# An attention and gated-MLP kernel whose written order follows rules with fixed numbers: the numbers now change stage by stage by a table

## The chip, the cores and the metric

The kernel runs on one core of a Trainium2 chip. Times are device microseconds; the profile is one profiled execution of the whole program. A core has five engines with queues of their own: PE (TensorE, matrix products), DVE (VectorE), ACT (ScalarE), POOL (GpSimd) and SP (SyncE, which here only starts transfers). Each runs its instructions in the order in which they were written and waits for the others by semaphores.

## The reference, cut to what matters

```python
# S = 2048, D = 512, H = 32 heads of 16, F = 1376, everything bf16
g = sigmoid((x * gate_w).sum(-1, keepdims=True))
qkv = (x @ wqkv)                       # split into q, k, v, 32 heads each
p = softmax(q @ k.T * 16 ** -0.5)      # per head, 2048 x 2048
a = (p @ v, heads joined) @ wo
b = ((x @ w_gate) * (x @ w_up)) @ w_down
out = g * a + (1 - g) * b
```

The softmax has 32 x 2048 x 2048 exponentials, which is what most of the kernel's work hangs on. There is no maximum taken off; the sums of the exponentials come out of the same products as the values, from a column of ones beside each head's values.

## The kernel before, in words

**Units.** The scores are cut into 2048 units of 128 keys x 512 queries of one head. They come in 32 groups `m` (8 times four heads, for each of 4 chunks of 512 queries), each of 16 key tiles times 4 heads. One unit fills one PSUM bank of 128 x 512. `score` (L1191) issues its four small matmuls of 64 rows x 32 columns (L1237), on the upper or the lower half of the rows of PE's array; two such packs on the two halves run beside each other.

**Two ways to take the exponential.** A unit is of kind "a" or "d", which `score` decides when it issues it.

- Kind "a": ACT reads the bank and writes bf16 exponentials to a cell of the SBUF tile PT (L1332, in `act_policy`, L1283). One pass takes two units where two neighbouring banks are ready, and else one.
- Kind "d": DVE adds a constant to the bank and writes int16 (L1474, in `dve_pass`, L1446). The score is scaled so that the integer's bits, read as bf16, are a coarse exponential. To make it finer the unit's cell is copied three times with an integer offset each (SH = 0, 32, 64, 96): on POOL (L1411) or on DVE (L1414), both in `run_shift` (L1395), for 512, 1024 or 2048 elements of a partition at once. The four cells are each multiplied with their own scaled copy of the values (CW), so that a "d" unit costs four times the value matmuls of an "a" unit.

**The value products.** `pv_pack` issues four matmuls of 64 rows x 32 columns (L1776) that add exponentials times values into one PSUM bank per group. When a group is complete, its bank is copied out, the sums are inverted and brought back by small transfers, and POOL multiplies (L1693) into OT.

**Fills.** All other products (transposing x, the projections k, q, v, the gate and up projections, the down projection, the output projection; L563, L567, L601) are "fills": they go to PE where it would otherwise not have work, and DVE takes their results out of PSUM. Cells of PT are used first for weights and x, later for exponentials as they come free.

**Who sets the order.** A planner runs when the program is written. It keeps a clock of its own with a fixed duration for each kind of instruction, and when an engine is free by that clock it asks the engine's policy (`dve_policy`, `act_policy`, `pool_policy`, `pe_policy`, `sp_policy`) for its next instruction. What is issued is put at the end of the engine's queue; the waits follow from the data. The chip knows nothing of the planner's clock; it only gets the order. The policies compare with numbers. Among those that the change touches:

- TA and TLO: up to how much ACT work is queued may PE issue a score for ACT, and below how much is "a" preferred to "d";
- DTH, DTH2, RQ, CD, DE, DK: how much DVE work may be queued, and how many cells must be free, for a "d" unit to be issued, and near which end of a group none is;
- AB, DB: which of the 8 PSUM banks are for "a" (below AB) and for "d" and fills (from DB);
- GM: with how many units ACT may make a pass, in which order they are tried; AW: how long ACT may wait for a second unit;
- WIN, SKEW: how far the scores may be taken out of order, and how far one half of PE may lead the other;
- CQ, CQ1, PW, SPL: when DVE takes a shift copy itself, when POOL does, and when a copy is split;
- CL, FP, PB, PL, PACE2, AHEAD, FB, EV, RES: when a fill goes ahead of the value products, how far one half leads in them, and when DVE empties a bank ahead of an exponential.

The last group's sums, the last product with wo and the output stand behind the planner's loop in a fixed order (L1998 to L2083).

## Time and the profile before

| | |
|---|---|
| median of 3 runs | 711.08 us (711.0 to 711.76) |
| the profiled execution | 711.66 us |
| its span in the trace | 709.9 us |
| granted clock of PE | 1.00 |
| PE, ACT, DVE, POOL busy | 99%, 97%, 92%, 60% of the span |

Busy time counts an instruction from its start to its end; where two overlap, as successive instructions on one engine do, the shared time counts once. "PEld" is the loading of PE's weights. A line such as "L1332 ACT ACTIVATE ... x740 | 684.6, 1055 | 9.3 <-..." gives a group's count, its busy time in us, the mean of one in ns, and the time for which the engine stood idle just before instructions of the group, with what ended it.

### The profile page before, as it was taken

What the parts mean: (1) busy time and instruction counts of PE and PEld (TensorE: products, weight loads), DVE (VectorE), ACT (ScalarE), POOL (GpSimd) and SP (SyncE); (2) the same over time, 40 slices, a digit from 0 to 9 for tenths busy, and PEclk for the clock granted to TensorE, in tenths of its full rate; (3) what the DMA queues carried; (4) which work ended last, traced back from release to release, by engine and by line L of the source; (5) the groups of instructions that cost most, each with busy time, mean ns of one, the idle gap of its engine ahead of it and who ended that gap; (6) DMA issues with size and microseconds to landing.
All of it is one profiled execution on the core that took longest, in us unless ns stands there. A gap on an engine that the chain in (4) does not pass through costs nothing.

```text
span 709.9 us, 47002 instructions
## 1 busy us (share of the span) xinstructions
PE 700.3 (99%) x21872; PEld 385.8 (54%) x21872; DVE 656.4 (92%) x1160; ACT 691.8 (97%) x757; POOL 429.4 (60%) x326
## 2 busy tenths in 40 slices
PE   8999999999999999999999999999999999999997
PEld 5555555555555556545555564545555555555553
DVE  5788999998999999999999999999999999998994
ACT  6989999999999999999999999999999999999997
POOL 3124767767455767456667477776546777772671
PEclk9999999999999999999999999999999999999999
DMA  8300111312012222212005221111104311120001
GB/s 248 80 9 9 28 26 36 72 38 57 23 27 50 66 68 46 53 38 62 22 9 120 48 54 34 31 53 37 46 6 96 83 38 57 38 73 9 16 19 39
DMA packets 77619, 34.86 MB, mean 49 GB/s; under 512 B 60784, under 2 KB 74480, under 8 KB 77424
## 3 DMA queue, kind: packets, MB, share of 16 engines
q1 hardware_dynamic: 76480, 31.34, 18.0%
q8 instruction: 171, 2.80, 1.6%
q10 hardware_dynamic: 944, 0.52, 0.2%
q14 instruction: 24, 0.20, 0.1%
HBM read 25.23 MB, written 2.35 MB: 39 GB/s over the span
## 4 chain that ended last, share of the span: by engine, by line
PE 91%; DVE 5%; DMA 1%; ACT 1%; SPq 1%; issue 1%; DVEq 0%
PE ps L1237 32%; PE ps L1776 31%; PE ps L567 27%; DVE PT L1474 2%; DMA gw<-in_gate_w_dram 1%; ACT PT L1332 1%; DVE PT L1414 1%; SPq L450 1%; PE ps L563 0%; DVE omg L834 0%; DVE KT L642 0%; DVE usb L918 0%; DVE VV L758 0%; PE ps L601 0%; PE ps L784 0%
## 5 line engine op out<-in xcount | busy, mean ns | idle before, releaser
L1332 ACT ACTIVATE PT<-ps 128x1024 bf16<-128x1024 f32 x741 | 685.1, 1054 | 9.3 <-PE ps L1237 4.3
L1776 PE MATMUL ps<-PT,VV 64*32 64x512 bf16 x7498 | 552.9, 377 | 1.1
L1411 POOL TENSOR_SCALAR PT<-PT 128x1024 int16<-128x1024 int16 (+1 forms) x284 | 395.7, 1410 | 209.1 <-DVE PT L1414 84.4
L1237 PE MATMUL ps<-QT,KT 64*32 64x512 bf16 x8192 | 477.4, 379 | 2.9 <-DVE PT L1474 1.1
L567 PE MATMUL ps<-PT 64*32 64x512 bf16 x5536 | 390.5, 377 | 0.4 <-DVE VV L758 0.2
L1474 DVE TENSOR_SCALAR PT<-ps 128x512 int16<-128x512 f32 x567 | 369.9, 683 | 14.8 <-PE ps L1237 9.5
L1776 PEld LDWEIGHTS ps<-PT,VV 64*32 64x32 bf16 x7498 | 189.0, 92 | 87.4 <-PE ps L1776 12.4
L1237 PEld LDWEIGHTS ps<-QT,KT 64*32 64x32 bf16 x8192 | 140.3, 89 | 152.2 <-ACT PT L1332 61.3
L567 PEld LDWEIGHTS ps<-PT 64*32 64x32 bf16 x5536 | 134.5, 92 | 64.7 <-DVE PT L1474 9.7
L1414 DVE TENSOR_SCALAR PT<-PT 128x2048 int16<-128x2048 int16 (+1 forms) x290 | 159.8, 594 | 5.8 <-PE ps L1776 5.1
L567 PE MATMUL ps<-wo,OT 64*32 64x512 bf16 x480 | 37.4, 377 | 0.1
L748 POOL TENSOR_SCALAR VV<-VV 128x528 bf16<-128x528 bf16 x17 | 10.7, 631 | 39.6 <-DVE VV L758 35.0
L933 DVE TENSOR_TENSOR PT<-ps,usb 128x512 bf16<-128x512 f32 (+1 forms) x44 | 30.0, 681 | 2.6 <-PE ps L567 2.5
L918 DVE CAST usb<-ps 128x512 bf16<-128x512 f32 (+1 forms) x44 | 30.0, 681 | 2.1 <-PE ps L567 2.1
L1693 POOL TENSOR_TENSOR OT<-oraw,rb 128x512 bf16<-128x512 f32 x16 | 20.5, 1278 | 18.4 <-DVE PT L1414 18.4
L1715 DVE COPY oraw<-ps 128x512 f32<-128x512 f32 x31 | 21.1, 682 | 1.0 <-PE ps L1776 0.9
L758 DVE CAST VV<-ps 128x512 bf16<-128x512 f32 x16 | 10.8, 688 | 7.3 <-PE ps L567 7.2
L567 PEld LDWEIGHTS ps<-wo,OT 64*32 64x32 bf16 x480 | 12.0, 92 | 7.0 <-DVE PT L1474 1.3
L642 DVE CAST KT<-ps 128x512 bf16<-128x512 f32 x16 | 11.0, 685 | 4.4 <-PE ps L1776 1.9
L982 DVE TENSOR_SCALAR bsb<-ps,omg 128x512 bf16<-128x512 f32 x16 | 11.9, 743 | 0.2 <-PE ps L567 0.2
L699 DVE TENSOR_SCALAR QR<-ps 128x512 bf16<-128x512 f32 x16 | 10.9, 683 | 0.5 <-PE ps L567 0.5
L626 DVE CAST PT<-ps 128x512 bf16<-128x512 f32 x14 | 8.9, 683 | 2.6 <-PE ps L601 2.6
(51 smaller groups left out, 78.8 us busy)
## 6 DMA issues: line engine op xcount, KB each, us to landing
PT<-in_B_w_up_dram SPq DMA_DIRECT2D x40, 128.0 KB, 3.0
PT<-in_B_w_gate_dram SPq DMA_DIRECT2D x40, 128.0 KB, 3.3
PT<-in_B_w_down_dram SPq DMA_DIRECT2D x20, 256.0 KB, 3.3
rb<-rscr SPq DMA_DIRECT2D x15, 256.0 KB
QT<-QR SPq DMA_DIRECT2D x124, 16.0 KB, 2.0
oraw<-oraw SPq DMA_DIRECT2D x60, 32.0 KB, 2.0
out_dram<-ost SPq DMA_DIRECT2D x14, 128.0 KB, 2.1
PT<-in_A_x_dram SPq DMA_DIRECT2D x3, 512.0 KB, 7.4
```

The lines of the kernel that those rows point to most:

```text
L567: o = pe.matmul(ps[32 * i : min(w, 32 * i + 32), bank, :], lhs(32 * i, min(w, 32 * i + 32))[q], rhs[q], start=s0, stop=s1, tile_position=( ...
L918: lambda v: v.tensor_copy(usb[0:w, n % 2, :], ps[0:w, bank, :]),
L933: lambda v: v.tensor_tensor(hT[0:w, f, :], ps[0:w, bank, :], usb[0:w, n % 2, :], ALU.mult),
L982: lambda v: v.tensor_scalar(bsb[:, tt, :], ps[:, bank, :], omg[:, t : t + 1], None, ALU.mult),
L1237: o_ = pe.matmul(ps[32 * i_ : 32 * i_ + 32, x, :], KT[64 * r : 64 * r + 64, b, kt * 128 + 32 * i_ : kt * 128 + 32 * i_ + 32], QT[64 * r : ...
L1332: lambda a: a.activation(span(PT, cs).bitcast(BF16), span(ps, bs), ACT.Exp, scale=ESC),
L1411: fn = lambda e: e.tensor_scalar(dst, src, 1.0, sh, ALU.mult, ALU.add)
L1414: fn = lambda e: e.tensor_single_scalar(dst, src, sh, ALU.add)
L1474: lambda v: v.tensor_scalar(span(PT, cs), span(ps, bs), IOFF, 0.0, ALU.add, ALU.max),
L1693: lambda g: g.tensor_tensor(OT[:, pair % 6, :], oraw[:, 0, :], rb[:, :], ALU.mult),
L1715: lambda v: v.tensor_copy(oraw[:, p, :], ps[:, bank, :]),
L1776: o_ = pe.matmul(ps[32 * j : 32 * j + 32, ob, :], v_ap(k, kt, 8 * b + 2 * j + p, p)[rows], PT[rows, cell, :].bitcast(BF16), start=f0, stop ...
```

## The change

The numbers that were constants of `_build` become attributes of an object `kn`, read by the same policies at the same places. A table TUNE lists, for times of the planner's clock, which of them take another value from then on; there are 59 entries from 10 to 670, and the loop applies them as its clock passes. No instruction is added to the kernel's repertoire, no tile, transfer or bank is added, and the planner's durations are the same. Its line numbers are 67 higher behind the table (L1332 becomes L1399), and 71 higher behind the loop.

```diff
-    DTH = 1.2
-    CQ = 3
...
+    kn = _Knobs()
+    kn.CD = 2
+    kn.DTH = 1.2
...
+    TUNE = [
+        (10.0, {"CL": 8, "FP": 1, "AB": 4, "DB": 3}),
+        (20.0, {"CQ": 6}),
+        (30.0, {"CD": 4}),
+        (40.0, {"DTH": 1.6, "WIN": 4, "CL": 12}),
+        (50.0, {"CD": 2, "DTH": 1.2, "WIN": 2, "CQ": 3, "FP": 0, "AB": 4, "DB": 4}),
+        (60.0, {"PB": 2, "EV": 1}),
+        (80.0, {"PL": 4, "AHEAD": 400}),
+        (90.0, {"DE": 3, "RES": 6}),
+        (100.0, {"CD": 1, "SPL": 12, "AHEAD": 80, "GM": (2,)}),
...
+        (300.0, {"CD": 0, "CQ1": 2, "PL": 8, "SKEW": 3}),
...
+        (360.0, {"CQ": 2, "CQ1": 2, "DE": 2, "SKEW": 3, "TLO": 0.6, "TA": 1.3, "FP": 1}),
...
+        (410.0, {"CD": 2, "WIN": 2, "CL": 12, "SKEW": 2, "TLO": 0.6, "TA": 1.6, "SPL": 12, "EV": 0, "GM": (3, 2, 1), "DK": 6}),
...
+        (590.0, {"DTH": 1.2, "DTH2": 0.6, "PW": 0.5, "AW": 0, "WIN": 2, "SKEW": 4, "TLO": 0.6, "TA": 2.0, "EV": 0}),
...
+        (650.0, {"PACE2": 0.95, "AB": 4, "DB": 3}),
+        (670.0, {"FP": 0}),
+    ]
+    seg = 0
...
         def high(fb):
-            return [x for x in fb if x >= DB]
+            return [x for x in fb if x >= kn.DB]
...
             t = heapq.heappop(events)
             while events and events[0] <= t + 1e-9:
                 heapq.heappop(events)
+            while seg < len(TUNE) and t >= TUNE[seg][0]:
+                for k_, v_ in TUNE[seg][1].items():
+                    setattr(kn, k_, v_)
+                seg += 1
             moved = True
```

The instructions of the two built programs differ in these counts; all others are the same:

| | before | after |
|---|---|---|
| ACT exponential, two units a pass / one unit | 740 / 1 | 727 / 6 |
| DVE exponential, one unit / two units | 567 / 0 | 584 / 2 |
| PE value matmuls (L1776) | 7498 | 7624 |
| DVE shift copies of 2048 / 1024 / 512 elements (L1414) | 158 / 126 / 6 | 151 / 132 / 4 |
| POOL shift copies of 2048 / 1024 / 512 elements (L1411) | 122 / 161 / 1 | 141 / 164 / 0 |

## The prediction

> **What bounds the kernel now.** I read the page's first part, the chain of waits, the groups by form, the waits of single engines, the busy time by stretch, and the timeline of the end.

> ```profile
> span 709.9 us, 47002 instructions
> PE 700.3 (99%) x21872; PEld 385.8 (54%) x21872; DVE 656.4 (92%) x1160; ACT 691.8 (97%) x757; POOL 429.4 (60%) x326
> PE 91%; DVE 5%; DMA 1%; ACT 1%; SPq 1%; issue 1%; DVEq 0%
> ```

> Three engines look full, and the chain of waits gives 91% of the span to PE. Both readings need testing. First the groups by form, with the count, the busy time and the mean of one:

> ```profile
> L1332 ACT ACTIVATE PT<-ps 128x1024 bf16<-128x1024 f32 x740 | 684.6, 1055 | 9.3 <-PE ps L1237 4.3 <-PE ps L1776 4.0 <-PE ps L567 0.4
> L1474 DVE TENSOR_SCALAR PT<-ps 128x512 int16<-128x512 f32 x567 | 369.9, 683 | 14.8 <-PE ps L1237 9.5 <-PE ps L1776 1.4 <-PE ps L567 0.2
> L1411 POOL TENSOR_SCALAR PT<-PT 128x2048 int16<-128x2048 int16 x122 | 231.2, 1898 | 107.1 <-DVE PT L1414 77.3 <-PE ps L1776 14.1 <-PE ps L1237 10.9
> L1411 POOL TENSOR_SCALAR PT<-PT 128x1024 int16<-128x1024 int16 x161 | 166.8, 1045 | 102.0 <-DVE PT L1474 71.9 <-PE ps L1776 15.4 <-DVE PT L1414 7.1
> L1414 DVE TENSOR_SCALAR PT<-PT 128x2048 int16<-128x2048 int16 x158 | 105.4, 691 | 0.7 <-PE ps L1776 0.4
> L1414 DVE TENSOR_SCALAR PT<-PT 128x1024 int16<-128x1024 int16 x126 | 59.3, 487 | 5.1 <-PE ps L1776 4.7
> ```

> ACT does almost nothing but the exponential: 740 passes over two score units each and one over a single unit, that is 1481 of the 2048 units; DVE's L1474 does the other 567. A pair takes 1055 ns, but successive passes overlap, so that each adds only 684.6/740 = 0.925 us.

> Now the stretches (time, PE, PEld, DVE, ACT, POOL busy with counts):

> ```profile
> 30.00:40.00 10.00, 10.00 (x359) 5.69 (x340) 7.54 (x20) 10.00 (x12) 1.26 (x2) 1.00 0.02 6
> 40.00:50.00 10.00, 9.66 (x300) 5.05 (x292) 9.57 (x23) 8.59 (x10) 2.91 (x5) 1.00 0.04 10
> 50.00:60.00 10.00, 10.00 (x324) 4.98 (x312) 6.50 (x16) 8.35 (x10) 0.87 (x2) 1.00 0.02 4
> 100.00:650.00 550.00, 547.49 (x17620) 304.41 (x17609) 528.36 (x912) 548.17 (x594) 358.97 (x257) 1.00 0.20 49
> 500.00:550.00 50.00, 50.00 (x1684) 28.41 (x1678) 48.36 (x85) 49.92 (x56) 26.89 (x20) 1.00 0.22 52
> ```

> From 100 to 650 us ACT is idle for 1.8 us of 550. PE is "busy" as well, but with 17620/550 = 32.0 matmuls per us, while between 30 and 40 us it did 35.9 and in the densest steady stretch 33.7. So PE has 5 to 12% left in the steady part. Who waits for whom says the same:

> ```profile
> PEld ps L1237 <- ACT PT L1332: 61.3, 278, 0.8
> ACT PT L1332 <- PE ps L1237: 4.3, 7, 1.2
> ACT PT L1332 <- PE ps L1776: 4.0, 5, 1.4
> ```

> The score matmuls wait 61.3 us for ACT to free a PSUM bank; ACT waits 8.7 us in all for PE (0.4 of it for L567, in the first group row). ACT is the bound, PE is what ACT's release sets going, and the chain runs through PE because each PE instruction has a predecessor there.

> **The change part by part.** The edit itself alters only numbers that the scheduler reads when the program is written; what changes on the chip is the order and four counts. They come from the order of instructions of the two built programs. Everything is made against the profiled execution, 711.66 us with a span of 709.9; it lies 0.58 above the median of 711.08.

> 1. *Units moved from ACT to DVE.* ACT's pair passes go from 740 to 727 and its single passes from 1 to 6, so 1460 units are left; DVE's go from 567 to 588 (584 single ones and two double ones). Thirteen pairs at 0.925 give -12.0 us. Five singles cost between half a pair, 0.46, and the whole duration of the only single one:

> ```profile
> L1332 ACT ACTIVATE PT<-ps x741: 673/1043/1180, 9.2 to 702.1; 128x1024 bf16<-128x1024 f32 x185, 128x512 bf16<-128x512 f32 x1
> ```

> That is 0.673. A pair overlaps its neighbour by 1.055 - 0.925 = 0.13, so I take 0.673 - 0.13 = 0.54, and +2.7 for five. Sum -9.3 us; bounds -8.7 (0.673 each) and -12.0 (singles free). Nearly all of it lies on the path, since in the steady part ACT has no idle time that would absorb it. [...]

> 2. *The start.* Four of the new singles are passes 33 to 40 of ACT. In the trace this is just ahead of ACT's only real starvation:

> ```profile
> 25.33 22.24 ACT L1332 ACTIVATE PT<-ps 128x1024 bf16<-128x1024 f32 x24 [0.38 <-PE ps L1237]
> 48.69 1.02 ACT L1332 ACTIVATE PT<-ps 128x1024 bf16<-128x1024 f32 x1 [1.12 <-PE ps L1776]
> 51.10 5.60 ACT L1332 ACTIVATE PT<-ps 128x1024 bf16<-128x1024 f32 x6 [1.38 <-PE ps L1776]
> ```

> There PE sets the pace. Up to the point where ACT has done 120 units, the new order has 20 matmuls fewer on PE and three more units done on DVE: 20/35.9 = -0.6 us. Bounds: 0 and the 3.1 us for which ACT sits idle between 40 and 60 us (1.41 and 1.65 in two rows above).

> 3. *More matmuls.* Each of the 21 units brings three shifted copies more, and with them 126 matmuls of L1776 in all (7498 to 7624; the scores and the fills keep their counts). At the steady 32.0 per us that would be 3.9 us if PE were the bound, and 0 if PE's spare rate hides them. Per 50 ACT passes (46.2 us) the densest part of the old order has 1580 matmuls and of the new one 1600, or 34.6 per us, still under 35.9. I take +0.5 for moments in which it is not hidden.

> 4. *DVE and POOL.* DVE gains 17 single units at 369.9/567 = 0.652 and two double ones at no more than 1.30, and loses in L1414 seven copies of 2048 elements (0.667 each) for six of 1024 (0.471) with two small ones less: +13.7 - 2.4 = +11.3 us. POOL gains 19 copies of 2048 (1.895) and 3 of 1024 (1.036): +39 us, on an engine that is 60% busy. Cost on the path 0, because ACT waits for neither by name; what covers it is DVE's idle time in the steady part, 550 - 528.4 = 21.6 us, and it shrinks to about half. If that cover is gone, see the second rival.

> 5. *The end.* In the profiled execution:

> ```profile
> 689.25 13.49 ACT L1332 ACTIVATE PT<-ps 128x1024 bf16<-128x1024 f32 x15
> 697.49 1.28 POOL L1693 TENSOR_TENSOR OT<-oraw,rb 128x512 bf16<-128x512 f32 x1 [3.77 <-DVE PT L1414]
> 701.74 1.91 PE L1776 MATMUL ps<-PT,VV 64*32 64x512 bf16 x20
> 703.59 1.04 PE L1998 MATMUL ps<-bsb,idt 128*128 128x512 bf16 x4
> 704.46 1.03 PE L2007 MATMUL ps<-wo,OT 128*128 128x512 bf16 x4
> ```

> ACT's last pass ends at 702.74, the rest takes 7.2 us. The new order puts nine packs of four value matmuls behind the start of the last pass instead of four, and the product on POOL that L2007 needs comes in the midst of them, not four passes ahead. Five packs at 35.9 matmuls per us are 0.6 us, if they do not run during the last pass; the product, begun at about ACT's end, would end 1.3 us later, and L2007 begins 1.7 us after that end now, so it is covered unless its transfer lands late. +0.4, bounds 0 and +1.3. The queue of SP carries the same transfers in slightly another order; SP's share of the chain is 1%, so nothing is put on it.

> Sum: 711.66 - 9.3 - 0.6 + 0.5 + 0.4 = 702.7 for an execution like the profiled one, 702.1 against the median, rounded 702.0. From the bounds alone: -12.0 - 3.1 gives 696.0, and -8.7 + 3.9 + 1.3 gives 707.6.

> **The rivals.** *PE is the bound after all* (0.07). The chain's 91% and PE's 547.5 of 550 speak for it. Then passes saved on ACT buy nothing and the 126 matmuls are paid in full: 711.08 + 3.9 = 715.0. It decides as soon as PE cannot exceed its 32.0 per us in the steady part; the forecast needs about (17620 + 100)/540.6 = 32.8 there. Against it stand the 35.9 and 33.7 above and the 61.3 us that PE waits for ACT.

> *DVE becomes the bound* (0.03), through the steady part. If DVE keeps its 21.6 us of waiting there and takes the 11.3 us on top, the time is 722.4; nothing is gained from the point where 9.4 us of DVE's added work cannot be hidden. For it: by busy time, 528.4 + 11.3 = 539.7 of 540.6 us would be taken. Against it: busy time counts the tail of an instruction that has no close follower.

> ```profile
> 301.97 0.60 DVE usb L918
> 306.08 0.60 DVE PT L933
> ```

> An equal read of 512 columns from PSUM adds 0.60 us to the chain, not 0.652, so 567 of them leave another 0.05 x 567 = 28 us. POOL could also block DVE: if each added copy on POOL held DVE up for its whole length, DVE would need 539.7 + 39 = 579 us in the steady part, and 711.08 + 29 = 740 would come out; of the 0.03, 0.01 is for that. [...] In the trace the waiting falls on POOL:

> ```profile
> POOL PT L1411 <- DVE PT L1414: 84.4, 59, 4.4
> ```

> None of DVE's named waits is for POOL, since the written order starts DVE's copies when POOL's are through.

> *The new order also takes ACT's remaining waits away* (0.15). A table made with look-ahead can place fills so that ACT's 8.7 us behind PE shrink. All of it gone would give 702.0 - 8.7 = 693.3, half 697.7. Against it: most of these waits lie in the first 60 us, where PE has no spare rate.

> *The saved passes come back as idle ACT time* (0.04): the time stays at 711, with ACT's busy time 9 us lower and its waits 9 us higher. The changed limits on how far scores run ahead (TA down to 1.3 in a middle stage) could do it; the trace of before cannot show it.

> **How the numbers follow.** The forecast has 0.71. About 0.2% is what a measurement here tells from no change, 1.4 us. Faster: 0.71 + 0.15 + half of the last rival, 0.88; same 0.02; slower 0.10 from the first two. The range: 697.0 takes in the lower bound of the sum but for its last microsecond and half of the third rival; 708.0 takes in the upper bound, 707.6. About 0.08 lies below and 0.12 above.

> **What would show it right or wrong.** Right: the group of ACT's pairs with 727 at about 0.925 each, busy near 675; ACT idle in the steady part under 4 us; PE at about 33 matmuls per us there; DVE's idle time there down to about 10 us with POOL at 465 to 470 busy; the work behind ACT's last pass 7 to 8 us long. Wrong: ACT idle for PE of over 10 us more (PE or handoff is the bound), DVE's L1474 as the main thing that PE waits for (DVE is), or pairs spaced 0.94 and more.

## The result and the profile after

The changed kernel took 702.65 us (median of 4 runs, 699.67 to 704.97), the kernel before 711.42 in the same session (711.0 to 711.91); the ratio is 0.9874, 95% interval 0.9833 to 0.9915. The prediction said 702.0 with 697.0 to 708.0. The profiled execution took 703.67 us, its span is 701.9. In three later sessions the kernel before had medians of 714.1 to 714.8, and the changed one, run in two of them, 707.8 and 706.65, ratios 0.9910 (0.9883 to 0.9938) and 0.9895 (0.9860 to 0.9931). The spread is new among these runs: 5 us between runs of the changed kernel, under 1 us for the kernel before. In the later ones the kernel before scatters too, by 2.8 to 4.2 us, and the changed one by 4.6 and 6.7.

The page of the changed kernel, its span, part 1 and the first line of part 4:

```profile
span 701.9 us, 47331 instructions
PE 692.5 (99%) x21994; PEld 384.4 (55%) x21998; DVE 660.2 (94%) x1176; ACT 684.1 (97%) x749; POOL 467.5 (67%) x347
PE 95%; DMA 1%; ACT 1%; SPq 1%; issue 1%; DVE 1%; DVEq 0%
```

Its groups by form (busy us, mean ns of one, idle before them):

```profile
L1399 ACT ACTIVATE PT<-ps 128x1024 bf16<-128x1024 f32 x727 | 674.6, 1050 | 7.9 <-PE ps L1304 5.7 <-PE ps L634 0.4 <-PE ps L1843 0.2
L1541 DVE TENSOR_SCALAR PT<-ps 128x512 int16<-128x512 f32 x584 | 379.8, 682 | 15.3 <-PE ps L1304 6.1 <-PE ps L1843 2.8 <-PE ps L634 1.9
L1478 POOL TENSOR_SCALAR PT<-PT 128x2048 int16<-128x2048 int16 x141 | 267.3, 1897 | 137.7 <-DVE PT L1481 96.1 <-PE ps L1843 24.5 <-PE ps L1304 10.7
L1481 DVE TENSOR_SCALAR PT<-PT 128x2048 int16<-128x2048 int16 x151 | 99.6, 688 | 0.5 <-PE ps L1843 0.4
L1481 DVE TENSOR_SCALAR PT<-PT 128x1024 int16<-128x1024 int16 x132 | 57.0, 451 | 2.2 <-PE ps L1843 1.7
```

ACT's pairs now cost 674.6/727 = 0.928 us each (0.925 before). DVE and POOL took their additional work, 660 and 467 us. The start, on ACT's timeline:

```profile
25.10 17.15 ACT L1399 ACTIVATE PT<-ps 128x1024 bf16<-128x1024 f32 x19 [0.38 <-PE ps L1304]
42.42 18.54 ACT L1399 ACTIVATE PT<-ps 128x1024 bf16<-128x1024 f32 x21 [0.17 <-PE ps L1304]
```

And the busy time by stretch, columns as before:

```profile
40.00:50.00 10.00, 10.00 (x336) 5.17 (x324) 9.32 (x22) 9.71 (x13) 3.46 (x6) 1.00 0.05 11
50.00:60.00 10.00, 10.00 (x316) 5.14 (x308) 9.06 (x17) 9.99 (x12) 5.68 (x5) 1.00 0.04 7
100.00:650.00 550.00, 546.29 (x17892) 304.61 (x17880) 531.05 (x923) 545.03 (x590) 391.50 (x275) 1.00 0.20 48
```

Two things stand out against the lines of before. Between 40 and 60 us ACT's idle time is 0.3 us where it was 3.1: the starvation is gone. From 100 to 650 us it is 5.0 where it was 1.8: something new takes time there. The starts of ACT's passes say how much. Back to back, two pairs start 0.905 us apart in both traces; what lies above that, by stretch, is this (worked out from the start times, us; time between two passes counts to the stretch in which the first one starts):

| | before | after | difference |
|---|---|---|---|
| first pass starts at | 9.2 | 9.3 | +0.1 |
| all passes at their closest spacing | 670.2 | 660.8 | -9.4 |
| above it, up to 100 us | 9.6 | 4.9 | -4.8 |
| above it, 100 to 650 us | 12.7 | 17.6 | +4.9 |
| above it, from 650 us on | 0.8 | 1.1 | +0.2 |
| from the last pass to the end | 7.1 | 8.1 | +1.0 |
| span | 709.9 | 701.9 | -8.0 |

What the 4.9 us are shows in what PE's weight loads wait for. "issue" is standing still without a semaphore that would hold it. First the kernel before, then the changed one (total us, times, longest):

```profile
PEld ps L1237 <- issue: 3.6, 8, 0.8
PEld ps L567 <- issue: 1.9, 5, 0.4
PEld ps L1776 <- issue: 1.2, 5, 0.3
```

```profile
PEld ps L1304 <- issue: 6.3, 13, 1.0
PEld ps L1843 <- issue: 4.6, 10, 1.1
PEld ps L634 <- issue: 4.0, 11, 0.6
PEld ps L1304 <- ACT PT L1399: 53.4, 239, 0.5
```

On the changed kernel's timeline two such stops look like this:

```profile
237.95 0.10 PEld L1304 LDWEIGHTS ps<-QT,KT 64*32 64x32 bf16 x3 [1.04 <-issue]
238.39 1.99 DVE L1541 TENSOR_SCALAR PT<-ps 128x512 int16<-128x512 f32 x3 [1.02 <-PE ps L634]
238.64 1.94 ACT L1399 ACTIVATE PT<-ps 128x1024 bf16<-128x1024 f32 x2 [0.72 <-PE ps L1304]
...
586.86 0.09 PEld L1843 LDWEIGHTS ps<-PT,VV 64*32 64x32 bf16 x1 [1.14 <-issue]
587.50 2.14 ACT L1399 ACTIVATE PT<-ps 128x1024 bf16<-128x1024 f32 x2 [0.73 <-PE ps L1304]
```

PE halts in the midst of a pack: one of four loads of the score pack is through, the other three come 1.04 us later; DVE and ACT then wait for it. Queue 8 of the page, of kind "instruction", has 172 packets of 16 KB here and 171 in the kernel before. PE's matmuls and weight loads, 43,992 and 43,744, come to 255.8 for each packet in both, so this queue is read as the one that carries PE's instructions, in blocks of 256 (128 matmuls and their weight loads). Counted over all halts of more than 250 ns after 20 us, at weight loads that wait for no semaphore:

```
                 halts   us in all   end of the halt, after the end of a packet (5%, median, 95%)
before             9        4.1      1.33  1.42  1.54 us
after             24       12.4      1.26  1.38  1.58 us
```

The weight loads at which the halts end stand 127 or 128 apart or multiples of it: number 6730, 6857, 6985, 7112, 7240 and 7367 in a row between 218 and 238 us. So each halt (but the last of the 24, 0.4 us behind the loop, 2.7 us after a packet) is at the border of a block of 256 instructions by this count, and ends 1.4 us (median) after the end of the packet before it. In a row of such halts one block follows another after 3.7 to 4.5 us, and the two packets that start closest to each other between 100 and 650 us are 3.27 us apart (3.33 in the kernel before). A block of 128 matmuls lasts 128/32.5 = 3.9 us at the steady rate.

Where two halts are one block apart (11 times), one packet starts between them: 1.1 to 2.0 us after PE has gone on at the first border. It takes 1.0 to 1.4 us, and PE goes on at the next border 1.2 to 1.5 us after its end. So in these rows the next block came only after PE had entered the one ahead of it, and this round trip of 3.7 to 4.5 us stands against the 3.9 us that a block lasts. Here PE runs beside the supply of its own instructions.

### The profile page after: what moved, and what is told of

Same layout as the page of the kernel before. It is cut to its first block, busy times and chain, and to the rows that moved or that the text cites. A ratio compares the mean times of both kernels' runs of the same rounds, so it can differ in the third digit from the quotient of the medians.

```text
span 701.9 us, 47331 instructions
## 1 busy us (share of the span) xinstructions
PE 692.5 (99%) x21994; PEld 384.4 (55%) x21998; DVE 660.2 (94%) x1176; ACT 684.1 (97%) x749; POOL 467.5 (67%) x347
## 4 chain that ended last, share of the span: by engine, by line
PE 95%; DMA 1%; ACT 1%; SPq 1%; issue 1%; DVE 1%; DVEq 0%
PE ps L1304 34%; PE ps L1843 34%; PE ps L634 26%; DMA gw<-in_gate_w_dram 1%; ACT PT L1399 1%; SPq L517 1%; PE ps L630 0%; DVE PT L1541 0%; PE ps L851 0%; PE ps L668 0%; PE ps L2078 0%; PE ps L2069 0%; DVE ost L2146 0%; DVEq L104 0%; DVE KT L709 0%
## 5 line engine op out<-in xcount | busy, mean ns | idle before, releaser
L1399 ACT ACTIVATE PT<-ps 128x1024 bf16<-128x1024 f32 (+1 forms) x733 | 677.4, 1047 | 7.9 <-PE ps L1304 5.7
L1843 PE MATMUL ps<-PT,VV 64*32 64x512 bf16 x7624 | 558.1, 377 | 1.9 <-issue 0.9
L1478 POOL TENSOR_SCALAR PT<-PT 128x1024 int16<-128x1024 int16 (+1 forms) x305 | 434.0, 1439 | 173.0 <-DVE PT L1481 101.9
L634 PE MATMUL ps<-PT 64*32 64x512 bf16 x5536 | 403.3, 377 | 0.3 <-issue 0.2
L1541 DVE TENSOR_SCALAR PT<-ps 128x512 int16<-128x512 f32 x586 | 382.2, 684 | 15.3 <-PE ps L1304 6.1
L1843 PEld LDWEIGHTS ps<-PT,VV 64*32 64x32 bf16 x7624 | 192.0, 92 | 98.0 <-PE ps L1843 13.5
L634 PEld LDWEIGHTS ps<-PT 64*32 64x32 bf16 x5536 | 138.4, 92 | 63.9 <-PE ps L634 6.6
L1481 DVE TENSOR_SCALAR PT<-PT 128x2048 int16<-128x2048 int16 (+1 forms) x287 | 150.9, 573 | 2.7 <-PE ps L1843 2.0
L634 PE MATMUL ps<-wo,OT 64*32 64x512 bf16 x480 | 35.1, 377 | 0.0
L634 PEld LDWEIGHTS ps<-wo,OT 64*32 64x32 bf16 x480 | 11.6, 91 | 5.0 <-DVE PT L1541 1.2
L709 DVE CAST KT<-ps 128x512 bf16<-128x512 f32 x16 | 10.9, 681 | 2.8 <-PE ps L630 1.6
```

Source lines behind the costliest of these rows:

```text
L634: o = pe.matmul(ps[32 * i : min(w, 32 * i + 32), bank, :], lhs(32 * i, min(w, 32 * i + 32))[q], rhs[q], start=s0, stop=s1, tile_position=( ...
L1399: lambda a: a.activation(span(PT, cs).bitcast(BF16), span(ps, bs), ACT.Exp, scale=ESC),
L1478: fn = lambda e: e.tensor_scalar(dst, src, 1.0, sh, ALU.mult, ALU.add)
L1481: fn = lambda e: e.tensor_single_scalar(dst, src, sh, ALU.add)
L1541: lambda v: v.tensor_scalar(span(PT, cs), span(ps, bs), IOFF, 0.0, ALU.add, ALU.max),
L1843: o_ = pe.matmul(ps[32 * j : 32 * j + 32, ob, :], v_ap(k, kt, 8 * b + 2 * j + p, p)[rows], PT[rows, cell, :].bitcast(BF16), start=f0, stop ...
```

## The experiments

In what follows theory S is that supply: the gain of the order is larger than 9 us, and a part of it is lost where PE asks for blocks faster than they come. Its rivals were that passes alone count, that the halts have another origin, and that PE's array bounds.

**The changed kernel again.** No edit.

> The changed kernel once more, for its spread (its four runs lie between 699.7 and 705.0 us, those of before within 0.9 us) and for a second profile. In the first profile PE stood still 24 times for over 250 ns with no semaphore to wait for (12.4 us in all, against 9 times and 4.1 us before), and each of these stops ended 1.2 to 1.6 us after the end of a 16 KB packet of PE's instruction queue. Theory S (supply of PE's instructions): the stops come at other places or in another number in each execution, and account for the spread; again some 20 of them, 8 to 14 us, with the same distance to a packet's end. Rival (a fixed property of the order): the same stops at the same times to within 1 us. Time 702.7, between 699 and 705.

707.8 us (704.6 to 711.3, 6 runs) against 714.14 (712.25 to 716.45). That is outside the 699 to 705 that I had written: both kernels took longer this time. 33 halts, 16.5 us, nine in ten of them 1.28 to 1.61 us after a packet's end. Of the 24 halts of the first profile 18 are at the same weight loads (3669, 3797, 4433, 6730 to 7367 among them); the others come or go, and their lengths differ. So the order fixes where PE runs out of margin, and the execution decides which blocks come late: theory S, and the source of the spread.

**The table's first five entries alone.**

```diff
     TUNE = [
         (10.0, {...}), (20.0, {...}), (30.0, {...}), (40.0, {...}), (50.0, {...}),
-        (60.0, {"PB": 2, "EV": 1}),
...
-        (670.0, {"FP": 0}),
     ]
```

> The table cut behind its entry at 50, so that the rules are those of before from there on; 736 pair passes and 4 single ones on ACT, 572 units on DVE. Theory P (only the number of ACT's passes counts): 4 pairs less and 3 singles more, -3.7 + 1.6 = -2.1, 709.3 us. Theory G (the start gained by itself, since ACT's waits before 100 us fell by about 4.5 us in the changed kernel): -2.1 - 4.5, about 704.8. Theory C (the chip follows the planner's clock, whose end is 6.8 us later than for before): 718.

718.55 us (717.6 to 722.22; ratio 1.0069, 1.0044 to 1.0094): 4.4 us slower than before in the same session, so neither theory P (2.1 us less) nor G (6.6 less) gives the time. In its profile, of the slowest execution (722.22 us), the start was gained all the same: above the closest spacing up to 100 us stand 5.0 us (9.6 before). But from 100 to 650 it is 22.8 us (12.7 before), with 14 halts of 7.8 us in all, and the end takes 13.8 us after the last pass instead of 7.1, where POOL's last product waits for the inverted sums, as a row of this run's timeline shows:

```profile
711.32 1.27 POOL L1706 TENSOR_TENSOR OT<-oraw,rb 128x512 bf16<-128x512 f32 x1 [8.78 <-DMA rb<-rscr]
```

**The table without them.**

```diff
     TUNE = [
-        (10.0, {"CL": 8, "FP": 1, "AB": 4, "DB": 3}),
-        (20.0, {"CQ": 6}),
-        (30.0, {"CD": 4}),
-        (40.0, {"DTH": 1.6, "WIN": 4, "CL": 12}),
-        (50.0, {...}),
         (60.0, {"PB": 2, "EV": 1}),
         ...
```

> The table without its five entries up to 50; the rules are those of before up to 60, and the table's from there on; 731 pairs and 10 singles on ACT, 576 units on DVE. Theory P: 9 pairs less, 9 singles more, -8.3 + 4.9 = -3.4, 708.0 us. Theory G: no gain at the start, and denser work on PE later, some 2 us dearer: 710. Theory C: the planner's end is 2.2 us earlier than for before, 709.2. The stops of PE without a semaphore: above 9.

718.27 us (713.89 to 722.99; ratio 1.0056, 1.0027 to 1.0086), 4.1 us slower than before, though ACT has nine pairs less and only nine single passes more. In its profile, of one of the fastest executions (714.2 us), 16.9 us lie above the closest spacing from 100 to 650 us, the end takes 10.1 us after the last pass, and there are 13 halts of 6.1 us in all (above 9, as expected). Theory P, 3.4 us less, falls with this run and the one before: the number of passes is what can be gained, not what is gained. It would fit both runs if the later entries suit only the state in which the first ones leave the planner; no run tests that by itself. Theory C, the planner's clock, had the sign right for the first run: 6.8 us more forecast, 4.4 more measured. That 718.55 meets the 718 of the forecast is luck, since the kernel before was 3 us slower beside it too. For the second run it had the sign wrong: 2.2 us less forecast, 4.1 more measured.

**Fewer instructions on PE, the order unchanged.**

```diff
-            for i in range((w + 31) // 32):
+            for i in range((w + 31) // 32 if s0 or s1 else 1):
```

> The changed kernel in the same order, but the fills' accumulation steps between the first and the last issue one of their four column tiles; some 3400 matmuls and as many weight loads fewer. It leaves out part of the projections' and the MLP's sums. A pack of one tile takes PE's rows as long as one of four (they run beside each other), so PE's order and the time that its array needs stay, and only the number of PE's instructions falls. Theory S: the stops of PE without a semaphore fall from 12 us to under 4, and the time by 4 to 9 us, to 694 to 699. Rival A (PE's array or the order bounds, and the stops are of another origin): 702.7 as before, stops unchanged.

695.71 us (695.36 to 696.17), 12.1 below the changed kernel in the same session, and the spread is 0.8 us instead of 6.7. Two halts remain (1.7 us), one of them the one behind the loop. Groups of this run by form:

```profile
L1399 ACT ACTIVATE PT<-ps 128x1024 bf16<-128x1024 f32 x727 | 671.1, 1056 | 3.6 <-PE ps L1304 2.6
L634 PE MATMUL ps<-PT 64*32 64x512 bf16 x2266 | 400.2, 378 | 0.1
```

Its steady stretch, and what PE's loads of the scores and the fills wait for without a semaphore:

```profile
100.00:650.00 550.00, 548.26 (x15218) 307.13 (x15209) 537.16 (x937) 549.05 (x598) 395.26 (x278) 1.00 0.20 48
```

```profile
PEld ps L1304 <- issue: 2.2, 3, 1.3
PEld ps L634 <- issue: 0.6, 2, 0.4
```

L634 has 2266 matmuls instead of 5536 and is busy for 400 us as before (403 in the changed kernel, by its page), since a pack's four tiles ran beside each other (rows of four of L634's matmuls last 0.39 to 0.40 us in the changed kernel's timeline, one matmul 0.376 in the median): the array's time, as the profile has it, is the same and the instructions are fewer. ACT is idle for 1.0 us of the 550, and its pairs are back at 671.1/727 = 0.923.

**The same in the order of before.**

> The kernel before, in its order, with the same matmuls left out as in the run with fewer PE instructions (some 3400, the middle accumulation steps of the fills; part of the projections' and the MLP's sums is missing). With this the two orders can be compared where PE's instructions come fast enough. Theory S: the kernel before loses less to the supply than the changed one: 711 on a chip like the first goes to 706 to 708 and its spread falls under 1 us; the distance to the changed order without stops (695.7) is then 11 to 13 us, more than the 9.3 of the passes, since the start is gained too. Rival (the table's gain is the passes alone): a distance of 9 us or less.

The edit is the same line in the kernel before. 709.9 us (709.47 to 710.25) against 714.34: ratio 0.9934 (0.9916 to 0.9952), no halt over 250 ns left, and its runs lie within 0.8 us where those of the kernel before lie within 2.8. I expected 706 to 708, from the first session's 711; here it is 4.4 below its own base. The two orders thus lie 709.9 - 695.7 = 14.2 us apart where the supply plays no part (two sessions, the kernel before at 714.14 and 714.34 in them). With all instructions in place they lie 6.3 and 8.1 us apart, in the two later sessions that had both. The supply takes back about half.

The profiles, one of each kernel, say where. Above the closest spacing from 100 to 650 us this run has 10.2 us and the run with fewer instructions in the new order 10.2 as well. So where the supply plays no part the orders do not differ there, and the +4.9 us of the first comparison are 7.4 that the supply costs the new order (17.6 less 10.2) less 2.5 that it costs the old one (12.7 less 10.2).

**Lighter transfers.**

```diff
-                    src[:, f * 128 : f * 128 + w].rearrange("(kt p) n -> p kt n", p=128),
+                    src[0:128, 0 : KD * w].rearrange("p (kt n) -> p kt n", kt=KD),
```

> The changed kernel with its 80 loads of up and gate weights taking 128 rows of 1 KB instead of 512 rows of 256 bytes, the same bytes in a quarter of the packets; the weights are then the wrong ones (the MLP's products are not the reference's), the order is the same. Theory S1 (the blocks of PE's instructions are late because they queue among the weights' small packets): stops without a semaphore fall from 24 to 33 down to under 15, time 3 to 7 us lower than the changed kernel. Theory S2 (the blocks' round trip itself is about as long as PE needs for a block): number and length of the stops stay, time within 2 us of the changed kernel.

706.13 us (703.89 to 707.34), 26 halts of 11.7 us in all; against the kernel before in the same session the ratio is 0.9888 (0.9863 to 0.9912), within what the changed kernel has (0.9874 to 0.9910). The trace has 45760 packets on the kernel's own queue instead of 76480. The weights' small packets are not what makes the blocks late. That leaves theory S2, which this run does not show by itself; the round trip measured between two halts, 3.7 to 4.5 us, does.

**Wider tiles for the fills.** A way to have fewer instructions with every sum complete:

```diff
-            for i in range((w + 31) // 32):
+            cw = 64                                # 128 in the second run
+            for i in range((w + cw - 1) // cw):
                 o = pe.matmul(
-                    ps[32 * i : min(w, 32 * i + 32), bank, :],
+                    ps[cw * i : min(w, cw * i + cw), bank, :],
...
```

> The changed kernel with each fill pack as two matmuls of 64 rows x 64 columns instead of four of 64 x 32; the computation is the reference's, the order is the same, and PE has some 3000 matmuls and 3000 weight loads fewer. Theory S, if tiles of two widths can stand beside each other at no cost: stops nearly gone, 696 to 698. Rival D (a change of the tile's width empties the array; the planner counts 0.13 us for the change between full and 64-row tiles): about 1500 packs of fills in 64 x 64, most between packs of 64 x 32; at 0.1 to 0.2 us for two changes each and two halves at once, 75 to 150 us more: 780 to 850.

> As the run with 64 x 64 tiles, with one matmul of 64 rows x 128 columns a fill pack; 4500 matmuls and weight loads fewer. Theory S without a cost for the width: 695 to 697. Rival D: as there, 780 to 850.

1597 us with 64 columns (at a granted clock of 0.70 in its profile, so no price is taken from it) and 1244.5 us with 128 columns (one run, clock 0.99): rival D in kind, but far above its 780 to 850. In the trace of the second the width changes 2660 times between the fills' packs and the others; against some 706 us that is 538 us more, 0.2 us for each. PE's weight loads stand still without a semaphore for 614 us there, 611 of them at a change of width. On its timeline:

```profile
586.95 0.10 PEld L1844 LDWEIGHTS ps<-PT,VV 64*32 64x32 bf16 x4 [0.23 <-issue]
586.95 0.40 PE L1844 MATMUL ps<-PT,VV 64*32 64x512 bf16 x4
587.28 0.09 PEld L635 LDWEIGHTS ps<-PT 64*128 64x128 bf16 x1 [0.23 <-issue]
587.28 0.39 PE L635 MATMUL ps<-PT 64*128 64x512 bf16 x1
587.60 0.11 PEld L1305 LDWEIGHTS ps<-QT,KT 64*32 64x32 bf16 x8 [0.23 <-issue]
587.60 0.41 PE L1305 MATMUL ps<-QT,KT 64*32 64x512 bf16 x8
587.62 0.10 PEld L1844 LDWEIGHTS ps<-PT,VV 64*32 64x32 bf16 x4
```

At the changes in these rows the next load comes 0.23 us after the one before it has ended, and the first matmul of the new width starts 0.07 us before the last one of the old width ends; L1844's loads, of the same width as L1305's, follow those after 0.02 us (587.60 and 587.62). That the array is emptied there, as rival D has it, was my estimate; the runs show the waits. ACT then waits for PE throughout:

```profile
L1400 ACT ACTIVATE PT<-ps 128x1024 bf16<-128x1024 f32 (+1 forms) x733 | 734.3, 1023 | 491.8 <-PE ps L1305 427.4 <-PE ps L1844 60.7 <-DVE PT L1482 0.5
```

At 0.2 us for each change, this run gives a reason for all small packs of this kernel to have one width.

**How the loss grows with the count.** In one session: the changed kernel, the edit of the fourth experiment with three and with two tiles instead of one, and the opposite, the first tile of each fill pack as two matmuls of 256 columns (its sums then differ from the reference's).

```diff
-            for i in range((w + 31) // 32):
+            for i in range((w + 31) // 32 if s0 or s1 else min(3, (w + 31) // 32)):   # 2 in the next run
```

```diff
-            for i in range((w + 31) // 32):
+            for i, lo, hi in [(0, 0, 256), (0, 256, 512)] + [(i, 0, 512) for i in range(1, (w + 31) // 32)]:
                 o = pe.matmul(
-                    ps[32 * i : min(w, 32 * i + 32), bank, :],
+                    ps[32 * i : min(w, 32 * i + 32), bank, lo:hi],
...
```

> The changed kernel on the chip of the three runs beside it, as their base: 21998 matmuls, 172 blocks of 256 instructions on PE. 702 to 708 us, 24 to 33 stops without a semaphore of over 250 ns, 12 to 17 us in all.

> The changed order; the middle accumulation steps of the fills leave out one of four column tiles (part of the projections' and the MLP's sums is missing): 20852 matmuls, 163 blocks. Theory S: a block costs time only where PE would be through with it before the next one is there, so the loss falls faster than the count; stops about 6 to 10, 4 to 5 us, and 5 to 7 us below the base. If the loss went with the count alone (12 us for the 28 blocks between the base and the run with one tile): 3.9 us below the base. Rival A (array or order): within 1 us of the base.

> As the run with three tiles, with two of four left out: 19658 matmuls, 154 blocks. Theory S: stops nearly gone (under 4), time within 1.5 us of the run with one tile, that is 9 to 11 us below the base. By the count alone: 7.7 us below. Rival A: within 1 us of the base.

> The changed order and the reference's computation; the first column tile of each fill pack is issued as two matmuls of 256 columns instead of one of 512, the same columns through the array with 1504 matmuls and weight loads more: 23502 matmuls, 184 blocks. Theory S: the densest stretches ask for a block every 3.4 us, which is as fast as any came; stops rise to 50 or more, 25 to 35 us in all, and the time by 10 to 20 us over the base. By the count alone: +5. Rival A: under 2 us more.

| blocks of 256 | halts over 250 ns | us in all | median us | runs from to |
|---|---|---|---|---|
| 144 (another session) | 2 | 1.7 | 695.71 | 695.36 to 696.17 |
| 154 | 2 | 0.8 | 696.48 | 696.03 to 697.06 |
| 163 | 11 | 4.8 | 698.97 | 698.22 to 699.3 |
| 172 (the changed kernel) | 30 | 14.7 | 706.65 | 704.42 to 709.02 |
| 184 | 57 | 36.2 | 741.76 | 741.04 to 742.65 |

From 144 to 154 blocks nothing is lost beyond 0.8 us between two sessions, from there on ever more: +2.5, +7.7, +35.1 us. That is theory S's shape; a loss by the count alone would be a straight line. The step from 163 to 172 is a little larger than the 5 to 7 expected. The last step is larger than the 10 to 20 expected, and halts account for 21.5 of its 35.1 us; what the rest is was not settled. In that run ACT waits for PE as a rule:

```profile
L1399 ACT ACTIVATE PT<-ps 128x1024 bf16<-128x1024 f32 (+1 forms) x733 | 686.5, 1033 | 35.8 <-PE ps L1304 26.9 <-PE ps L1843 5.1 <-PE ps L634 0.7
```

No run with the reference's computation beat the changed kernel.

## Why the prediction was right, point by point

The time was right (702.0 against 702.65), and two of its five terms, the second and the third, were wrong in size by about the same amount with opposite signs. That they cancel is luck. In the later sessions the changed kernel lay 6.3 and 8.1 us below the kernel before, where 9.1 was forecast, and one of the signs named beforehand missed: ACT's idle time in the steady part is 5.0 us, not under 4.

1. *Units moved.* -9.3 expected, -9.4 at the closest spacing. The single passes cost less than I took: (677.4 - 674.6)/6 = 0.47 us by the busy times of the page and of the pairs, close to half a pair. This term holds as what the order can gain; the second and third experiments show that it comes only if nothing else takes its place.

2. *The start.* -0.6 expected with bounds of 0 and 3.1; it was -4.8 up to 100 us. I had counted 20 matmuls less up to one point and called PE's rate the limit. What the new order did was to spread ACT's and PE's work so that ACT never ran dry: the gap before the passes at 48.69 and 51.10 is closed, and the bound of 3.1, ACT's idle time, left out the stretched spacing of passes that still overlap. It is not the supply's doing: in the fifth and the fourth experiment, where that plays no part, the same stretch has 8.4 and 4.5 us. With it the third rival, which I gave 0.15, came true for the start, for the very stretch for which I had argued against it.

3. *More matmuls.* +0.5 expected with bounds of 0 and 3.9; it was +4.9 from 100 to 650 us. The step that failed is the rate: I took 35.9 matmuls per us, from a stretch of 10 us, for what PE can do, and compared it with an average. The new order's densest part asks for 34.6, and there it is not the array that ends last but the next block of instructions. PE itself was not short of speed: between the ends of the halts at 218.0 and 237.95 us it took 637 weight loads in 19.9 us. Of these, 3.0 us are halts, which makes 37.7 loads per us while it ran and 31.9 with the halts. The 126 matmuls themselves are one block. What counts is that the order is denser: without the halts, 128 weight loads in a row between 100 and 650 us take 3.78 us in the median where they took 3.90, and less than 3.5 us in 17% of all places where it was 8%. The fourth and fifth experiments give the supply its size in their sessions: 12.1 us of the changed kernel's time (707.8 less 695.71) and 4.4 of the kernel before's.

4. *DVE and POOL.* DVE's busy time is 660.2 (656.4 + 11.3 = 667.7 by the prediction), and POOL's 467.5 lies in the 465 to 470 expected. DVE's idle time in the steady part is 19 us, not the 10 I expected. Part of it is that the copies of 1024 elements cost less than I counted: 132 take 57.0 us where 126 took 59.3. The traces show why: some of DVE's copies are held up by POOL. A copy that begins while POOL is in an instruction, with more than 150 ns of it to come, ends 0.28 us (1024 elements) or 0.55 us (2048) after that instruction's end; begun with POOL free it takes 0.42 or 0.68 us in all. In the kernel before, a copy of 1024 begun at 464.30 us, in a copy on POOL that lasted from 463.56 to 465.46, took 1.44 us. Of copies begun like this there are 32 before and 29 after. In all the copies of 1024 are held up by 8.6 us before and 4.5 after, those of 2048 by 1.0 and 0.8. The exponential's reads of PSUM show nothing of it: L1541 takes 0.682 us beside a POOL instruction and 0.685 without one. So the prediction's reason, that DVE's copies start when POOL's are through, does not hold for all of them (59 of the 290 before begin while POOL is in an instruction), and the hold stands in their length, not in a wait. But it became smaller, by 4.2 us, with 38 us more on POOL: that each added copy would hold DVE up for its whole length, the dearest case of the second rival, was my assumption and is not what the traces show. The idle time covers the additional work; the rival falls. POOL, for its part, still waits for DVE's copies (L1478's first wait above).

5. *The end.* +0.4 expected with bounds of 0 and 1.3; +1.0 measured. The product on POOL was covered, as said; the nine packs were not:

```profile
684.22 9.58 ACT L1399 ACTIVATE PT<-ps 128x1024 bf16<-128x1024 f32 x11
691.47 1.27 POOL L1760 TENSOR_TENSOR OT<-oraw,rb 128x512 bf16<-128x512 f32 x1 [1.61 <-DVE PT L1481]
692.88 2.80 PE L1843 MATMUL ps<-PT,VV 64*32 64x512 bf16 x44
695.83 0.81 PE L2069 MATMUL ps<-bsb,idt 128*128 128x512 bf16 x3 [0.16 <-issue]
```

ACT ends at 693.80, the eleven last packs of L1843 at 695.68, and L2069 starts 2.03 us after ACT's end instead of 0.85.

The first rival (PE is the bound, 0.07) was nearer to the truth than I gave it. PE did 17892/550 = 32.5 matmuls per us in the steady part, between its 32.0 and the forecast's 32.8; the chain's 95% for PE was a hint, and the waiting of 53 us for ACT did not exclude that PE is short elsewhere. The fourth rival, idle time that comes back on ACT, came true for about 3 us.

## What to carry to other kernels

Here the denser order was worth what the supply of PE's instructions let through: 6.3 and 8.1 us with all of them in place, 14.2 where the supply played no part. For another engine that is fed with many small instructions (here 32.5 matmuls and as many weight loads per us), look for standing still without a semaphore, and for its distance to the instruction queue's packets. Take a rate from the stretch that lasts, not from the best 10 us. The parts of a table of settings are not a sum of gains: here each of two parts alone was 4 us slower than none.
